# Five loads for each w_in tile, and three neighbouring PSUM banks for each attention chunk

## Chip, core and metric

The kernel runs on one core of a Trainium2 chip. The metric is device time in microseconds. The kernel before the change was run three times: 589.63, 589.65 and 592.54 us, median 589.65 us. All inputs and the output are float32 for the attention part and float64 bit patterns for the two weight matrices, which the kernel reads as pairs of int32 words and turns into float32 itself.

## What is computed

A linear attention with a decay per channel (batch 4, 8 heads, 768 positions, 48 channels a head), whose output, 3072 rows of 384 columns, goes through a two-layer network with the gate h * cos(h):

```python
for t in range(S):
    kt, vt, rt = k[:, :, t], v[:, :, t], r[:, :, t]
    cur = einsum('bhd,bhe->bhde', u[None] * kt, vt)
    y[:, :, t] = einsum('bhd,bhde->bhe', rt, state + cur)
    state = w[None, :, :, None] * state + einsum('bhd,bhe->bhde', kt, vt)
x = y.transpose(0, 2, 1, 3).reshape(B * S, H * D)      # 3072 x 384
h = x @ w_in                                           # 384 x 2048
out = (h * cos(h)) @ w_out                             # 2048 x 384
```

The order of x's 384 columns is free as long as the rows of w_in stand in the same order, since h sums over them. The kernel uses that freedom: x is built transposed, in three thirds of 128 columns, and each third is made of four groups of 32 partitions.

## The kernel before, in words

**Attention.** The sequence is cut into 24 chunks of 128 positions (`chunk`, L631). A chunk loads k, r and v (one DMA each, L647 and L665, pieces of 192 bytes), multiplies r, k and u on POOL (L742, L750, L793), transposes k and r on PE (L711), copies the transposes out with the decay (L768, L779, L788), makes the scores A of eight heads (L818, into two PSUM banks), masks them into SBUF (L824), and makes x transposed from the carried state (L839) and from A and v (L850). It makes k times v for the next state too (L863; the state is updated in L915 to L918). x leaves PSUM twice: ACT rounds it to the reduced type of the matmuls (`xh`, L899), DVE takes the rest (`xl`, L903). Twelve chunks are done before or around the first step of the network (`EARLY = 12`), the others between later steps. The late ones load k and r a second time in another layout (L670), so that DVE can transpose them.

**Banks.** PSUM has eight banks of 512 float32 per partition. Banks 0 to 2 hold output sums and, early, the transposes; 3 to 5 hold h; 5 to 7 serve the attention. An early chunk takes its banks one by one from a pool of five (`B_EARLY`, banks 3 to 7): two for A, then two for x, and one for k times v.

**Network.** 128 steps: a step is one of 16 tiles f of 128 hidden columns for one of eight blocks of 384 rows of x. It has nine matmuls for h (L230: each product is made of three, from high and low parts), then ACT, DVE, ACT, DVE, ACT and DVE in turn (L241, L244, L247, L1017, L1020, L1023) for the gate, and nine matmuls into the output sums (L236). The first four blocks walk over f in groups (f 0 to 1, 2 to 4, 5 to 9, 10 to 15), so that the weights can come in meanwhile; their partial sums are added in DRAM by DMAs from POOL (L1065).

**Weights.** `conv` (L526) turns one tile into high and low parts: f has a w_in tile and a w_out tile, 393 KB of raw words each. A tile is loaded into one of three raw buffers (`R_raw`; the third is r's space, free after the early chunks), converted by ACT L552, DVE L560 and L572, POOL L583, ACT L588 and DVE L593. The raw buffer is free after L583. The w_out tile is one DMA (L461). The w_in tile is eight (L446): x's column order puts two runs of DRAM rows, 16 or 32 rows each and far apart, into neighbouring partitions, so the outermost dimension of the source has two entries:

```python
ap=[[(c1 - c0) * rl, 2], [rl, 16 * n], [1, 2 * P]]
```

In the second half the weights are read once more to look at their range (L456, one DMA for a w_in tile, in the matrix's own row order: 128 rows outermost).

**What sets the order.** Every piece of work is an `op` with an engine, a due time, a cost and buffers. `Plan.order` lays them out by these numbers, and each engine then executes its list strictly in that order. SP issues all loads and the plain stores, one after the other, so a DMA that waits for a free buffer holds up those behind it. Before the first step PE gets dummy matmuls (L1081) where the plan sees a gap.

Of the kernel before, what the change touches and what calls it, by code (L numbers as in the profile page):

```python
# [9 lines left out]
F32 = mybir.dt.float32  # L10
# [153 lines left out]
def kernel(  # L164
# [85 lines left out]
    with ExitStack() as actx:  # L250
# [3 lines left out]
        both = banks.tile([P, 2, 512], F32, name="both")  # L254
        bank = [Tile(both[:, i]) for i in range(2)]
        bank += [Tile(banks.tile([P, 512], F32, name=f"bank{i}")) for i in range(2, 8)]
# [3 lines left out]
        B_TR = [Tile(both)]  # L260
        B_WARM = bank[2]
# [71 lines left out]
        def start_dve():  # L333
# [12 lines left out]
            lambda: nc.sync.dma_start(wr[:, :, 0:D], w.rearrange("(p j) d -> p j d", j=2)),  # L346
# [58 lines left out]
        def tab_copy():  # L405
            pt = b_tab().rearrange("q (p j d) -> q (p j) d", p=NP, j=2)
            nc.scalar.copy(dec_k, pt[:, :, 0:D])
# [26 lines left out]
        def load_raw(i, raw, by_x=False):  # L434
            f, part = divmod(i, 2)
            if part == 0 and by_x:
                rl = 2 * DFF
                for kk in range(NK):
                    g = 0
                    while g < 4:  # L440

                        first = x_columns(kk, g)
                        n = 2 - len(first) + 1
                        (h0, skip0), (h1, skip1) = (x for i in range(n) for _, x in x_columns(kk, g + i))
                        c0, c1 = h0 * D + max(skip0, 0), h1 * D + max(skip1, 0)
                        nc.sync.dma_start(  # L446
                            raw()[32 * g : 32 * (g + n)].rearrange("p (kk f) w -> p kk (f w)", kk=NK)[:, kk],
                            bass.AP(
                                tensor=w_in_w.tensor,
                                offset=w_in_w.offset + c0 * rl + f * P * 2,  # L450
                                ap=[[(c1 - c0) * rl, 2], [rl, 16 * n], [1, 2 * P]],
                            ),
                        )
                        g += n
# [57 lines left out]

        def x_columns(kk, g):

            j, m, which = (
# [3 lines left out]
            )[kk][g]  # L519
            one, two = 4 * m + j, 4 * m + j + 2  # L520
            return (((0, (one, 0)),), ((0, (two, 16)),), ((0, (one, 32)), (16, (two, -16))))[which]
# [86 lines left out]
        for t in range(2):  # L608
            for j in range(2):
                for g in range(4):  # L610
                    some = [(*x, j, kk - j, g) for kk in range(NK) for _, x in x_columns(kk, g) if x[0] % 2 == j]
                    PARTS.append(some[t])

# [17 lines left out]
        def chunk(i, due, xbuf):  # L631
            b, c = i % B, i // B
            first = i < RAW_K
            bk = B_EARLY if i < EARLY else B_ATT
# [6 lines left out]
            Ap = [Buf(bk) for _ in range(2)]  # L641
            A = [Buf(R_A) for _ in range(2)]
            xp = [Buf(bk) for _ in range(2)]
            zp = Buf(bk)

            def load(buf, src):
                return lambda: nc.sync.dma_start(  # L647
                    buf()[:, :, 0:D], src[b, :, c * C : (c + 1) * C, :].rearrange("h t d -> t h d")
                )

# [10 lines left out]
            def rn():  # L661
                return heads(rb) if late else rb()[:, :, 0:D]

            def load_r():
                nc.sync.dma_start(rn(), r[b, :, c * C : (c + 1) * C, :].rearrange("h t d -> t h d"))  # L665

            def load_s(buf, src):
                def part(m, q, n_q, p, n_p, n):
# [5 lines left out]
                            offset=src.offset + ((b * H + 2 * p + j) * S + c * C + 4 * q) * D + d0,  # L674
                            ap=[[4 * D, n_q], [2 * S * D, n_p], [1, n]],
# [73 lines left out]
            def decay_k():  # L749
                n2.tensor_tensor(kb()[:, :, 0:D], kb()[:, :, 0:D], dec_k, op=ALU.mult)  # L750
# [482 lines left out]
```

## Time and profile before

| | |
|---|---|
| median of three runs | 589.65 us |
| the profiled execution | 589.45 us |
| its span, first to last instruction | 587.7 us |
| mean granted TensorE clock | 0.955 |
| PE, DVE, ACT, POOL busy | 527.6, 395.6, 328.4, 178.2 us |
| chain that ended last | PE 63%, DMA 17%, SPq 7%, DVE 5% |

How to read it: PE is TensorE's matmuls and PEld its weight loads, DVE is VectorE, ACT ScalarE, POOL GpSimd; SPq is the queue of SyncE that issues DMAs. "out<-in" names the tile written and those read, "x9" a count. In a row on windows each engine's busy time stands with its number of instructions, then PEclk (the clock that TensorE was granted, 1.00 is full), the mean busy share of the 16 DMA engines, and GB/s. A busy PE is not a PE at full rate, since the ends of matmuls are modelled and a slow clock makes them longer. The chain of waits is followed back from the last instruction; a DMA's piece in it runs from the start of its issue to its landing.

### The profile page before, as it was taken

Reading aid. Unit: us, or ns where it says so; the run is one execution under the profiler, and the core shown is the slowest. Engines: PE = TensorE matmul, PEld = TensorE weight load, DVE = VectorE, ACT = ScalarE, POOL = GpSimd, SP = SyncE. Lnnn points to the kernel's source line nnn. Section 1 sums busy time; section 2 is a strip of 40 time slices with the busy share of each in tenths; the row PEclk is TensorE's granted clock in tenths of the full one; section 3 lists DMA queues with packets and bytes.
Section 4 is the critical chain, followed back from the end, with each engine's and each line's share of the span. In section 5 each row is a group of like instructions: output and inputs, shape, how many; then the busy total and the mean of one; then the engine's idle time right before and its main releaser. Section 6 shows DMA issues by size and latency. Waiting matters only on the chain.

```text
span 587.7 us, 12700 instructions
## 1 busy us (share of the span) xinstructions
PE 527.6 (90%) x4721; PEld 490.9 (84%) x4721; DVE 395.6 (67%) x820; ACT 328.4 (56%) x841; POOL 178.2 (30%) x186
## 2 busy tenths in 40 slices
PE   8979857778668796999999999999999999999994
PEld 5757647667667696999999999999999999999994
DVE  5759865664666485745677688768777877776552
ACT  3768744653545364555456657655755676565442
POOL 6566322123333133411150445043043313300000
PEclk9989959979788987999999999999999999999998
DMA  9687324345344445632536678345726662501001
GB/s 143 113 143 131 72 81 128 107 142 127 87 102 106 105 102 124 124 45 38 95 70 118 124 166 198 83 121 122 190 81 163 163 155 86 150 3 40 2 1 45
DMA packets 114984, 61.66 MB, mean 105 GB/s; under 512 B 78433, under 2 KB 110818, under 8 KB 114914
## 3 DMA queue, kind: packets, MB, share of 16 engines
q1 hardware_dynamic: 109586, 53.50, 37.4%
q0 software_dynamic: 5184, 7.08, 8.6%
q8 instruction: 38, 0.62, 0.5%
q14 instruction: 32, 0.26, 0.1%
q10 hardware_dynamic: 144, 0.20, 0.1%
HBM read 48.96 MB, written 11.80 MB: 103 GB/s over the span
## 4 chain that ended last, share of the span: by engine, by line
PE 63%; DMA 17%; SPq 7%; DVE 5%; POOL 3%; issue 2%; ACT 1%; DVEq 0%; POOLq 0%; ACTq 0%
PE bank L230 26%; PE both L236 18%; PE bank L236 9%; DMA raw<-in_moe_w_in_dram 8%; SPq L446 7%; DMA r_all<-in_moe_w_in_dram 4%; PE bank L818 3%; PE bank L850 3%; DMA r_all<-in_r_dram 2%; DMA raw<-in_moe_w_out_dram 2%; PE bank L839 1%; POOL f L583 1%; DMA r_all<-in_moe_w_out_dram 1%; DMA k<-in_k_dram 1%; PE bank L863 1%
## 5 line engine op out<-in xcount | busy, mean ns | idle before, releaser
L230 PE MATMUL bank<-xh,w_in_hi 128*128 128x384 f32 x384 | 132.5, 345 | 6.8 <-ACT w_in_hi L588 4.1
L230 PE MATMUL bank<-xh,w_in_lo 128*128 128x384 f32 x384 | 131.3, 342 | 1.6 <-DVE w_in_lo L593 1.6
L230 PE MATMUL bank<-xl,w_in_hi 128*128 128x384 f32 x384 | 131.2, 342 | 0.0
L1023 DVE TENSOR_TENSOR gl<-f,gh 128x384 fp32r<-128x384 f32 (+1 forms) x132 | 78.6, 599 | 30.2 <-ACT gh L1020 29.9
L241 ACT ACTIVATE qi<-bank 128x384 int32<-128x384 f32 (+1 forms) x132 | 62.8, 479 | 60.1 <-PE bank L230 59.6
L247 ACT ACTIVATE f<-f 128x384 f32<-128x384 f32 (+1 forms) x132 | 67.3, 513 | 44.6 <-DVE f L244 43.0
L244 DVE SCALAR_TENSOR_TENSOR f<-bank,qi 128x384 f32<-128x384 f32 (+1 forms) x132 | 70.9, 540 | 29.5 <-ACT qi L241 29.1
L236 PE MATMUL both<-w_out_hi,gh 128*128 128x384 f32 x256 | 89.1, 348 | 1.4 <-DVE f L1052 1.1
L1017 DVE TENSOR_TENSOR f<-bank,f 128x384 f32<-128x384 f32 (+1 forms) x132 | 70.9, 540 | 27.3 <-ACT f L247 25.6
L1020 ACT CAST gh<-f 128x384 fp32r<-128x384 f32 (+1 forms) x132 | 65.8, 501 | 42.0 <-DVE f L1017 35.8
L236 PE MATMUL both<-w_out_hi,gl 128*128 128x384 f32 x256 | 88.7, 346 | 0.0
L236 PE MATMUL both<-w_out_lo,gh 128*128 128x384 f32 x256 | 88.3, 345 | 0.0
L230 PEld LDWEIGHTS bank<-xh,w_in_hi 128*128 128x128 f32 x384 | 74.2, 193 | 8.8 <-ACT w_in_hi L588 4.5
L230 PEld LDWEIGHTS bank<-xh,w_in_lo 128*128 128x128 f32 x384 | 73.9, 193 | 2.2 <-DVE w_in_lo L593 2.2
L230 PEld LDWEIGHTS bank<-xl,w_in_hi 128*128 128x128 f32 x384 | 74.1, 193 | 0.0
L236 PE MATMUL bank<-w_out_hi,gl 128*128 128x384 f32 x128 | 45.5, 356 | 20.1 <-DVE gl L1023 20.1
L808 ACT ACTIVATE A<-ident,a 128x128 f32<-128x128 f32 x192 | 59.5, 390 | 4.4 <-DVE a L799 4.2
L236 PE MATMUL bank<-w_out_hi,gh 128*128 128x384 f32 x128 | 45.8, 358 | 11.9 <-ACT f L1050 6.8
L730 POOL TENSOR_TENSOR kT<-kT,decT_k 112x512 f32<-112x512 f32 x12 | 15.7, 1311 | 128.5 <-DVE kT L725 78.4
L236 PEld LDWEIGHTS both<-w_out_hi,gh 128*128 128x128 f32 x256 | 49.5, 193 | 3.1 <-DVE f L1052 1.9
L236 PEld LDWEIGHTS both<-w_out_hi,gl 128*128 128x128 f32 x256 | 49.7, 194 | 0.0
L236 PEld LDWEIGHTS both<-w_out_lo,gh 128*128 128x128 f32 x256 | 49.7, 194 | 0.0
(104 smaller groups left out, 802.6 us busy)
## 6 DMA issues: line engine op xcount, KB each, us to landing
raw<-in_moe_w_out_dram SPq DMA_DIRECT2D x22, 384.0 KB
out_dram<-f POOLq DMA_DIRECT2D x36, 192.0 KB, 5.5
raw<-in_moe_w_in_dram SPq DMA_DIRECT2D x13, 384.0 KB
k<-in_k_dram SPq DMA_DIRECT2D x24, 192.0 KB
v<-in_v_dram SPq DMA_DIRECT2D x24, 192.0 KB
out_dram<-f SPq DMA_DIRECT2D x23, 192.0 KB
r_all<-in_moe_w_out_dram SPq DMA_DIRECT2D x10, 384.0 KB
raw<-in_k_dram SPq DMA_DIRECT2D x31, 96.0 KB
```

The costliest lines, as they stand in the source:

```text
L230: nc.tensor.matmul(ph, a, b_, start=(i == 0), stop=(i == len(mm) - 1))
L236: nc.tensor.matmul(acc, a[:, ts], b_[:, f, :], start=(first and i == 0), stop=(last and i == 2))
L241: nc.scalar.activation(qi, ph, AF.Copy, scale=INV_2PI, bias=0.25)
L244: nc.vector.scalar_tensor_tensor(q, ph, INV_2PI, qi, op0=ALU.mult, op1=ALU.subtract)
L247: nc.scalar.activation(q, q, AF.Sin, scale=TWO_PI, bias=0.5 * math.pi)
L446: nc.sync.dma_start(raw()[32 * g : 32 * (g + n)].rearrange("p (kk f) w -> p kk (f w)", kk=NK)[:, kk], bass.AP(tensor=w_in_w.tensor, offset ...
L808: nc.scalar.activation(A[j]()[:, p, :], ident, AF.Copy, scale=ab()[:, h : h + 1])
L818: nc.tensor.matmul(cube(Ap[j])[:, p, :], kT()[ps, p, :], rT()[ps, p, :], start=True, stop=True)
L850: nc.tensor.matmul(xv(i)[G * g : G * g + G, at, :], vb().rearrange("q h d -> q (h d)")[:, e0 : e0 + G], A[j]()[:, p, :], start=(not c and ...
L1017: nc.vector.tensor_tensor(g()[:, cs], ph()[:, cs], q()[:, cs], op=ALU.mult)
L1020: nc.scalar.copy(gh()[:, cs], g()[:, cs])
L1023: nc.vector.tensor_tensor(gl()[:, cs], g()[:, cs], f32(gh())[:, cs], op=ALU.subtract)
```

## The change

1. x gets a new column order (`x_columns`). Head h sits in half h // 4 of the partitions instead of h % 2. Each w_in tile is loaded by five DMAs, with 64 or 32 partitions as the outermost dimension; two of them carry one third of x, three of them two thirds.
2. All eight banks are one PSUM tile, and a chunk has three neighbouring ones: banks 2 to 4 for odd early chunks up to the ninth, otherwise 5 to 7. The second and third hold A at first; then the three hold a third of x each, in columns 0 to 127. The product of k and v stands in the first of them, in columns 128 to 319.
3. x leaves PSUM in one ACT and one DVE instruction of 128x384, instead of three each.
4. k and r of early chunks are loaded in two DMAs each, four heads a piece (`load_p`), so that the pairs of heads for PE's transposes lie side by side.
5. The dummy matmuls are twice as many with half the columns, in columns 384 to 511 of bank 2.

```diff
-        B_EARLY = bank[5:8] + bank[3:5]
+        B_EARLY = bank[5:8] + bank[2:5]
...
-                rl = 2 * DFF
-                for kk in range(NK):
-                    g = 0
-                    while g < 4:
-                        first = x_columns(kk, g)
-                        n = 2 - len(first) + 1
...
-                                ap=[[(c1 - c0) * rl, 2], [rl, 16 * n], [1, 2 * P]],
...
+                def rows(p0, n, kk, n_kk, c0, dc):
+                    rl = 2 * DFF
+                    dims = [[rl, n], [dc * rl, n_kk], [1, 2 * P]]
+                    nc.sync.dma_start(
+                        raw()[p0 : p0 + n].rearrange("p (kk f) w -> p kk (f w)", kk=NK)[:, kk : kk + 2 * n_kk - 1 : 2],
+                        bass.AP(
+                            tensor=w_in_w.tensor,
+                            offset=w_in_w.offset + c0 * rl + f * P * 2,
+                            ap=dims if n_kk > 1 else [dims[0], dims[2]],
+                        ),
+                    )
+                rows(32, 64, 0, 2, 0, 320)
+                rows(0, 32, 0, 2, 160, 64)
+                rows(96, 32, 0, 2, 128, 64)
+                rows(0, 64, 1, 1, 64, 0)
+                rows(64, 64, 1, 1, 256, 0)
...
-            bk = B_EARLY if i < EARLY else B_ATT
+            b0 = 2 if i % 2 and i < EARLY - 1 else 5
...
-            Ap = [Buf(bk) for _ in range(2)]
+            xp = [Buf([t]) for t in bank[b0 : b0 + 3]]
+            Ap = xp[1:]
...
-            xp = [Buf(bk) for _ in range(2)]
-            zp = Buf(bk)
+            zp = xp[0]
+            x_all = psum[:, b0 : b0 + 3, 0:C]
...
+            def load_p(buf, src):
+                def go():
+                    for j in range(2):
+                        nc.sync.dma_start(
+                            buf()[:, j::2, 0:D],
+                            src[b, j * NP : (j + 1) * NP, c * C : (c + 1) * C, :].rearrange("h t d -> t h d"),
+                        )
+                return go
...
             def x_high():
-                for rows, kk, src in x_parts():
-                    nc.scalar.copy(xbuf()[0][rows, kk], src)
+                nc.scalar.copy(xbuf()[0], x_all)
             def x_low():
-                for rows, kk, src in x_parts():
-                    nc.vector.tensor_tensor(xbuf()[1][rows, kk], src, f32(xbuf()[0])[rows, kk], op=ALU.subtract)
+                nc.vector.tensor_tensor(xbuf()[1], x_all, f32(xbuf()[0]), op=ALU.subtract)
...
-            wp = B_WARM.ap[:, 0:256].rearrange("q (a b) -> q a b", a=2)
-            for _ in range(n):
-                nc.tensor.matmul(wp, warm, warm[:, None, :].to_broadcast([P, 2, P]), start=True, stop=True)
+            for _ in range(2 * n):
+                nc.tensor.matmul(B_WARM, warm, warm, start=True, stop=True)
```

The plan lays the lists out anew. On SP, which issues the loads, this is where the first two early w_in tiles after f = 0 stand before the change: behind the last load of the twelve early chunks (names: k and v are the chunk's tiles, r_all holds r, raw the weights' words).

```order
L647 DMA k_86<-in_k_dram 128x8x48
L665 DMA r_all<-in_r_dram 128x8x48
L647 DMA v_89<-in_v_dram 128x8x48
L446 DMA raw_117<-in_moe_w_in_dram 64x1x256
L446 DMA raw_117<-in_moe_w_in_dram 32x1x256 x2
L446 DMA raw_117<-in_moe_w_in_dram 64x1x256 x2
L446 DMA raw_117<-in_moe_w_in_dram 32x1x256 x2
L446 DMA raw_117<-in_moe_w_in_dram 64x1x256
```

And this is the same place with the change: the two tiles (raw_111 and raw_112) stand between the loads of the last three chunks, five issues each instead of eight.

```order
L442 DMA raw_111<-in_moe_w_in_dram 64x2x256
L442 DMA raw_111<-in_moe_w_in_dram 32x2x256 x2
L442 DMA raw_111<-in_moe_w_in_dram 64x256 x2
L659 DMA k_78<-in_k_dram 128x4x48 x2
L659 DMA r_all<-in_r_dram 128x4x48 x2
L651 DMA v_81<-in_v_dram 128x8x48
L659 DMA r_all<-in_r_dram 128x4x48 x2
L442 DMA raw_112<-in_moe_w_in_dram 64x2x256
L442 DMA raw_112<-in_moe_w_in_dram 32x2x256 x2
L442 DMA raw_112<-in_moe_w_in_dram 64x256 x2
```

So the tiles of f = 1 and 2 are asked for earlier, and the last loads of k, r and v come after them.

On DVE, in the stretch in which weights arrive while steps run, three instructions of a step's gate (L244, L1025, L1031) alternate with three of a tile's conversion (L560, L572, L593). With the change they stand there like this (gl and gh are the gate's parts, f any scratch tile, psum a bank):

```order
L244 SCALAR_TENSOR_TENSOR f_100<-psum,qi_106 128x384
L1060 COPY f_99<-psum 128x384
L1031 TENSOR_TENSOR gl_109<-f_102,gh_107 128x384
L560 TENSOR_SCALAR f_98<-r_all 128x384
L1025 TENSOR_TENSOR f_100<-psum,f_100 128x384
L572 SCALAR_TENSOR_TENSOR f_98<-r_all,f_98 128x384
L593 TENSOR_TENSOR w_out_lo<-f_103,w_out_hi 128x384
```

Before the change the list reads much the same there:

```order
L244 SCALAR_TENSOR_TENSOR f_104<-bank_80,qi_112 128x384
L560 TENSOR_SCALAR f_105<-raw_117 128x384
L1023 TENSOR_TENSOR gl_116<-f_107,gh_114 128x384
L572 SCALAR_TENSOR_TENSOR f_105<-raw_117,f_105 128x384
L593 TENSOR_TENSOR w_out_lo<-f_109,w_out_hi 128x384
L1017 TENSOR_TENSOR f_104<-bank_80,f_104 128x384
```

One tile's conversion goes with one step in both; an L560 that waits for a load holds up the gate instructions behind it.

More of the change, by code (lines that the diff above doesn't have):

```diff
@@ L252 @@
         banks = actx.enter_context(tc.tile_pool(name="banks", bufs=1, space=PSUM))
-        both = banks.tile([P, 2, 512], F32, name="both")
-        bank = [Tile(both[:, i]) for i in range(2)]
-        bank += [Tile(banks.tile([P, 512], F32, name=f"bank{i}")) for i in range(2, 8)]
+        psum = banks.tile([P, 8, 512], F32, name="psum")
+        bank = [Tile(psum[:, i]) for i in range(8)]
         B_ACC, B_H, B_ATT = bank[0:3], bank[3:5], bank[5:8]
         B_HX = bank[3:6]
-        B_EARLY = bank[5:8] + bank[3:5]
-        B_TR = [Tile(both)]
-        B_WARM = bank[2]
+        B_EARLY = bank[5:8] + bank[2:5]
+        B_TR = [Tile(psum[:, 0:2])]
+        B_WARM = bank[2].ap[:, 384:512]
         def ring(name, n, shape, dtype):
@@ L513, in x_columns @@
         def x_columns(kk, g):
-            j, m, which = (
[3 rows of a table removed]
+            return (
[3 rows of a table added]
             )[kk][g]
-            one, two = 4 * m + j, 4 * m + j + 2
-            return (((0, (one, 0)),), ((0, (two, 16)),), ((0, (one, 32)), (16, (two, -16))))[which]
         def conv(i, due, behind=None):
@@ L610 @@
                 for g in range(4):
-                    some = [(*x, j, kk - j, g) for kk in range(NK) for _, x in x_columns(kk, g) if x[0] % 2 == j]
+                    some = [(*x, kk, g) for kk in range(NK) for _, x in x_columns(kk, g) if x[0] // NP == j]
                     PARTS.append(some[t])
+        PARTS = [(*x, x[2:] not in [y[2:] for y in PARTS[:n]]) for n, x in enumerate(PARTS)]
         last_A = [None]
@@ L741, in chunk @@
                 c0,
-                lambda: n0.tensor_tensor(heads(mb), rn(), kb()[:, :, 0:D], op=ALU.mult),
+                lambda: n0.tensor_tensor(
+                    split(heads(mb)), split(heads(rb)) if late else in_turn(rb), in_turn(kb), op=ALU.mult
+                ),
                 [l_r, l_k],
@@ L846, in mm_x @@
                         )
-                for n, (h, skip, i, at, g) in enumerate(PARTS):
-                    p, j = divmod(h, 2)
+                for h, skip, kk, g, new in PARTS:
+                    j, p = divmod(h, NP)
                     e0 = h * DP + skip
                     nc.tensor.matmul(
-                        xv(i)[G * g : G * g + G, at, :],
+                        xp[kk]()[G * g : G * g + G, 0:C],
                         vb().rearrange("q h d -> q (h d)")[:, e0 : e0 + G],
                         A[j]()[:, p, :],
-                        start=(not c and n < 8),
+                        start=(not c and new),
                         stop=True,
```

69 lines of the change are left out of this document (27 added, 42 removed), and 6 rows, old and new, of the table b_fine.

## The prediction

> **What bounds the kernel now.** I read the slices of the page first, then windows, then waits and the chain. PE is short of full from the second slice to the sixteenth (up to about 235 us), its granted clock dips in the same stretch, and the DMA engines are far from full there; afterwards PE is at 9 throughout.
>
> ```profile
> PE   8979857778668796999999999999999999999994
> PEclk9989959979788987999999999999999999999998
> DMA  9687324345344445632536678345726662501001
> ```
>
> The windows put numbers on it: 76.4 to 232 us, from the last product of the last early chunk to the end of the waits, and 340 to 400 us for comparison.
>
> ```profile
> 76.40:232.00 155.60, 113.81 (x559) 106.57 (x552) 92.52 (x193) 76.17 (x173) 46.00 (x44) 0.87 0.42 108
> 340.00:400.00 60.00, 60.00 (x540) 57.01 (x528) 47.25 (x97) 37.45 (x100) 20.45 (x18) 1.00 0.58 136
> ```
>
> In the first, 559 matmuls take 155.6 us; in the second, 540 take 60, among them the short ones of late chunks. What the matmuls of a step cost at full clock is in the chain:
>
> ```profile
> 241.16 1.06 PE both L236 x6
> 243.81 1.56 PE bank L230 x9
> ```
>
> That is 0.173 us for one of L230 (0.177 for L236), so 559 need 559 x 0.173 = 96.9 us. The other 58.7 us are waiting and half clock: PE is idle for 155.6 - 113.8 = 41.8 us, and a mean clock of 0.87 means half speed for a quarter of the time. PE waits in that stretch for the gate's last steps, but those stand on ACT and DVE behind conversions, and the conversions wait for w_in:
>
> ```profile
> PE bank L236 <- DVE gl L1023: 20.1, 8, 6.5
> PE bank L236 <- ACT f L1050: 6.8, 2, 4.1
> ACT raw L552 <- DMA raw<-in_moe_w_in_dram: 32.3, 8, 7.1
> DVE f L560 <- DMA raw<-in_moe_w_in_dram: 16.6, 5, 7.2
> ```
>
> So the loads of w_in set the pace. Their issues on SP, the first and the last of this stretch and one in between, and one load of the range check (L456), which fetches a tile of the same size from the same matrix:
>
> ```profile
> 58.80 4.95 SPq L446 DMA_DIRECT2D raw<-in_moe_w_in_dram  x8
> 89.50 7.38 SPq L446 DMA_DIRECT2D raw<-in_moe_w_in_dram  x8
> 214.50 5.74 SPq L446 DMA_DIRECT2D r_all<-in_moe_w_in_dram  x8
> 386.27 0.37 SPq L456 DMA_DIRECT2D raw<-in_moe_w_in_dram  x1
> ```
>
> From 58.8 to 214.5 us 14 tiles f come in, one in 11.1 us. What the DMA engines do while only w_in loads are in flight, and while the check's load is:
>
> ```profile
> 66.00:68.00 2.00, 2.00 (x70) 1.52 (x74) 1.82 (x7) 0.80 (x2) 0.00 (x0) 1.00 0.14 48
> 388.20:389.20 1.00, 1.00 (x7) 1.00 (x6) 0.56 (x1) 0.80 (x2) 1.00 (x2) 1.00 0.80 274
> ```
>
> With eight loads outstanding the engines are busy to 0.14, which is 2.2 of 16, at 48 GB/s; the same kilobyte rows in the check's order reach 0.80 and 274 GB/s. A w_in tile of 393 KB takes 393/48 = 8.2 us of those two engines, and what is queued behind it there waits too. The two differ in the source's outermost dimension: two runs of rows against 128 rows.
>
> **w_in's loads.** The new loads have 64 or 32 rows outermost, so I expect them to use the engines as the check does. [...]
>
> What a load takes from issue to landing, and the same for w_out tiles, which are 128 rows outermost, once free and once behind w_in loads, is in the chain:
>
> ```profile
> 62.55 0.62 SPq L446
> 63.22 6.71 DMA raw<-in_moe_w_in_dram
> 76.22 2.82 DMA raw<-in_moe_w_out_dram
> 107.42 7.43 DMA raw<-in_moe_w_out_dram
> ```
>
> I take 2.82 us for the landing of the last of five. A w_in tile then saves 3 issues of 0.62 + 0.05 us, 2.0 us, and 6.71 - 2.82 = 3.9 us; a w_out tile behind it up to 7.43 - 2.82 = 4.6 us. Three raw buffers serve 28 tiles in 155.7 us, so one is held 16.7 us; less the mean of 5.9 and 4.6 (5.2 us) it is 11.5 us, and 14 f's come in 14 x 2 x 11.5 / 3 = 107 us, 48 us less.
>
> What is late next in that stretch: PE can't go below 96.9 us. DVE is busy for 92.5 us there, and the change takes nothing from it, since the shorter work on x lies before 76.4 or after 232 us. The highest share of DVE in the windows above at which PE doesn't wait is 47.25/60 = 0.79; at that share 92.5 us need 117 us. So the stretch comes out between 97 and 117 us. I take 112, nearer to DVE's bound, since in DVE's list each step's three gate instructions alternate with three of a conversion. Gain: 155.6 - 112 = 43.6 us. The half clock goes with the long waits.
>
> **The early chunks (up to 76.4 us).** The first w_in tile is loaded amid the loads of k, r and v. Windows of that time and of just before, and a load of r there and before in the chain:
>
> ```profile
> 24.90:32.40 7.50, 6.78 (x149) 5.28 (x145) 4.55 (x11) 3.81 (x13) 0.38 (x1) 1.00 0.53 118
> 15.00:20.00 5.00, 5.00 (x114) 3.51 (x110) 3.38 (x9) 4.14 (x14) 4.54 (x6) 1.00 0.78 134
> 18.07 4.02 DMA r_all<-in_r_dram
> 25.64 6.76 DMA r_all<-in_r_dram
> ```
>
> The engines lose 7.5 x (1 - 0.53/0.78) = 2.4 us; that comes back. Against it, two more w_in tiles now stand ahead of the last chunks' loads: 786 KB at 134 GB/s, 5.9 us. But two steps' h are then done before the last chunk's products, 18 x 0.173 = 3.1 us that the next stretch need not do. Net: -2.4 + 5.9 - 3.1 = +0.4 us; from -2.4 to +5.9.
>
> Splitting k and r adds 24 issues on SP. One costs 0.37 to 0.51 us, and SP has waits for buffers on such loads to hide them:
>
> ```profile
> 56.80 0.37 SPq L647 DMA_DIRECT2D k<-in_k_dram  x1
> 58.19 0.51 SPq L647 DMA_DIRECT2D v<-in_v_dram  x1
> SPq L647 <- PE bank L850: 13.9, 8, 3.3
> ```
>
> 24 x 0.44 = 10.6 us against 13.9 us in this group alone: nothing, and 10.6 us if that cover is gone.
>
> **Banks.** A chunk now holds three banks from its first product of A until x and the state are out, and every second chunk needs the same three. From the chain:
>
> ```profile
> 37.54 2.02 PE bank L818 x15
> 42.66 1.16 PE bank L818 x16
> 44.42 1.01 PE bank L850 x32
> ```
>
> One chunk's A starts at 37.54, the next one's at 42.66, so chunks come every 5.1 us and a set must be free after 10.2. The first chunk's x is done at 45.43, and x leaves in 0.49 + 0.55 us (below): held 8.9 us. It fits, so 0; each us over 10.2 would cost half a us a chunk. [...]
>
> **x out of PSUM.** Three instructions become one. Today's, and two of 384 columns from a bank:
>
> ```profile
> L899 ACT CAST xh<-bank 128x256 fp32r<-128x256 f32 x24 | 8.8, 365 | 7.6 <-PE bank L850 7.0 <-DVE xl L903 0.6
> L899 ACT CAST xh<-bank 128x128 fp32r<-128x128 f32 x24 | 6.4, 266 | 0.6
> L903 DVE TENSOR_TENSOR xl<-bank,xh 128x256 fp32r<-128x256 f32 x24 | 9.9, 415 | 4.1 <-ACT xh L899 4.1
> L903 DVE TENSOR_TENSOR xl<-bank,xh 128x128 fp32r<-128x128 f32 x24 | 7.0, 292 | 0.4
> L241 ACT ACTIVATE qi<-bank 128x384 int32<-128x384 f32 x126 | 61.5, 488 | 59.6 <-PE bank L230 59.1
> L1017 DVE TENSOR_TENSOR f<-bank,f 128x384 f32<-128x384 f32 x126 | 69.5, 552 | 27.3 <-ACT f L247 25.6
> ```
>
> The third, of 64x128, is priced like the 128x128: ACT goes from 0.365 + 2 x 0.266 = 0.90 to 0.49 us, DVE from 0.415 + 2 x 0.292 = 1.00 to 0.55: 0.41 and 0.45 us a chunk. Twelve chunks lie where PE never waits (340 to 400 us above): nothing. In the early ones it shortens the hold, which has room: nothing, at best 6 x 0.86 = 5 us. The dummy matmuls have as many columns as before and stand in planned gaps: nothing.
>
> **Sum**, against the profiled execution's 589.45 us (0.2 below the median): 589.45 - 43.6 + 0.4 = 546.2, so **546 us**.
>
> **Rivals.**
>
> (a) The raw buffers stay the bound. If landing and hold shrink by half as much as priced, 14.1 us a buffer, 14 f's take 132 us instead of 107; the stretch ends some 22 us later than forecast: 568 us. For it: L552 and L560 are in-order and POOL's L583 stands behind stores; against it: those queues are late today because the loads are.
>
> (b) The loads don't spread, and only the issues go. The engines then still need 8.2 us a tile at 48 GB/s; 3 issues less give up to 14 x 2.0 = 28 us if all lie on the path and nothing if the transfer covers them: 561 to 589, middle 575 us. Against it: 0.80 busy in the check's load of the same rows.
>
> (c) Slower: two sets of banks hold up the early chunks. It decides where a set is held over 10.2 us; to eat the whole gain it must be held over 17.5 us. At 18.5 us twelve chunks lose 12 x 8.3 / 2 = 50 us, which gives 596 us. Against it: 8.9 us above. For it: a chunk's end waits for ACT and DVE, which also serve other chunks and conversions.
>
> **How the numbers follow.** Forecast 0.67, (a) 0.20, (b) 0.08, (c) 0.05. A measurement of this kernel can tell about 0.5% (3 us) from no change. Of (b) 0.03 lies within that, so faster is 0.67 + 0.20 + 0.05 = 0.92, same 0.03, slower 0.05. The range's low end is the stretch at PE's bound with the early gain: 589.45 - 58.7 - 2.4 = 528. Its high end takes in (a): 568 us and 2 for its rounding, 570. Outside lie (c), most of (b), and part of (a).
>
> **What would show it.** Right: with w_in loads in flight the DMA share is several times 0.14; a w_in tile has five issues, some 3.3 us in all, and lands about 3 us after the last; PE at 9 and clock near 1.0 from about 85 us on; the steps reach the state of 232 us by about 190; idle time before L552 and L560 mostly gone; 340 us to the end as before. Wrong: windows at 48 GB/s again (b); PE still waiting for gl with L552 idle for DMA (a); the last L850 of an early chunk far beyond 80 us (c). If DVE is at 0.9 or more in that stretch, 112 was too high; if PE waits for gl with DVE at 0.7 and no load late, the order itself is the limit, and the forecast's mechanism falls short.

## The result and the profile after

| | before | after |
|---|---|---|
| median | 589.94 us (4 runs) | 534.90 us (4 runs, 534.28 to 537.02) |
| ratio, 95% interval | 1 | 0.9065, 0.9028 to 0.9101 |
| profiled execution, its span | 589.45, 587.7 us | 535.15, 533.2 us |
| mean granted clock | 0.955 | 0.992 |
| PE, DVE, ACT, POOL busy | 527.6, 395.6, 328.4, 178.2 us | 512.1, 387.9, 318.8, 180.0 us |

Faster by 55 us where 43 were forecast; the time lies in the range, on its low side. The slices of the page show where it came from: PE is at 9 from the sixth slice on, but for the eleventh at 8 (a slice is 13.3 us; before, it was at 9 from the seventeenth), and the clock stays at 9 after the fifth.

```profile
PE   7997799999899999999999999999999999999995
PEclk9998899999999999999999999999999999999999
```

The same stretch in the view of windows, once over its old length and once up to where nearly all weights are in. The columns are the length, then busy time with instruction count of PE, PEld, DVE, ACT and POOL, then clock, DMA share and GB/s.

```profile
76.40:232.00 155.60, 153.92 (x949) 150.77 (x948) 127.82 (x249) 105.00 (x237) 61.17 (x60) 1.00 0.58 132
76.40:178.00 101.60, 99.92 (x640) 96.77 (x639) 92.73 (x185) 73.83 (x168) 43.71 (x43) 1.00 0.62 154
83.00:84.00 1.00, 1.00 (x52) 0.80 (x56) 0.79 (x2) 0.43 (x1) 1.00 (x1) 1.00 0.54 182
```

Where 559 matmuls took 155.6 us, 949 are done now. In the first 101.6 us DVE is busy for 92.7 us, about as long as in 155.6 us before, at a share of 0.91, and PE still hardly waits. The third row is a microsecond in which loads of one w_in tile alone are in flight (the one issued from 81.17 us on, below): 182 GB/s at a DMA share of 0.54, where 48 GB/s at 0.14 stood before.

SP's timeline has these w_in tiles: f = 3 before the change, then f = 3, 4 and 15 with it:

```profile
82.64 4.95 SPq L446 DMA_DIRECT2D r_all<-in_moe_w_in_dram  x8
```

```profile
73.11 3.12 SPq L442 DMA_DIRECT2D raw<-in_moe_w_in_dram  x5
81.17 2.89 SPq L442 DMA_DIRECT2D r_all<-in_moe_w_in_dram  x5
166.81 2.92 SPq L442 DMA_DIRECT2D raw<-in_moe_w_in_dram  x5
```

A tile now takes 2.89 us to issue where SP isn't held up, instead of 4.95. From f = 3 to f = 15 one w_in tile is asked for every 7.8 us (73.11 to 166.81), where it was 11.0 (82.64 to 214.50); the prediction's sum over the raw buffers gave 107 us for 14, 7.7 each. In the table of waits L552's wait for w_in is nearly gone (the first row, up to 180 us; before, 32.3 us), and two waits are new (the second row over the whole span, the third up to 180 us):

```profile
ACT raw L552 <- DMA raw<-in_moe_w_in_dram: 1.3, 1, 1.3
DVE zc L925 <- ACT xh L908: 12.9, 10, 2.0
PE psum L1088 <- DVE xl L911: 2.8, 3, 2.4
```

The second is the state's update waiting for ACT's copy of x, which reads the same bank; the third is a dummy matmul behind x's other copy. The chain of waits runs through PE for 85% of the span (63% before), and in the stretch it is step after step without a gap:

```profile
97.69 1.58 PE psum L236 x9
99.27 1.56 PE psum L230 x9
```

Two marks in PE's timeline are needed below, the last product for x of an early chunk (L850 before, L868 now; the row gives least, middle and greatest ns, then first and last start) and the 33rd step of the network, which ends the old stretch. First before, then after:

```profile
L850 PE MATMUL bank<-A,v x32: 421/421/421, 74.8 to 76.4; 128*32 128x128 f32 x32
L230 PE MATMUL bank<-xh,w_in_hi x3: 522/522/522, 231.4 to 233.3; 128*128 128x384 f32 x3
```

```profile
L868 PE MATMUL psum<-A,v x32: 272/273/298, 83.5 to 84.3; 128*32 128x128 f32 x32
L230 PE MATMUL psum<-xh,w_in_hi x3: 332/336/337, 178.8 to 179.9; 128*128 128x384 f32 x3
```

The first goes from 76.4 to 84.3 us, the second from 231.4 to 178.8. What follows the second takes 356.3 us before (587.7 - 231.4) and 354.4 now (533.2 - 178.8).

### The profile page after: what moved, and what is told of

Same layout as the page of the kernel before. It is cut to its first block, busy times and chain, and to the rows that moved or that the text cites. A ratio compares the mean times of both kernels' runs of the same rounds, so it can differ in the third digit from the quotient of the medians.

```text
span 533.2 us, 12662 instructions
## 1 busy us (share of the span) xinstructions
PE 512.1 (96%) x4790; PEld 485.3 (91%) x4790; DVE 387.9 (73%) x772; ACT 318.8 (60%) x793; POOL 180.0 (34%) x186
## 4 chain that ended last, share of the span: by engine, by line
PE 85%; DVE 7%; issue 2%; ACT 2%; DMA 2%; SPq 1%; POOL 0%; DVEq 0%; ACTq 0%; POOLq 0%
PE psum L236 36%; PE psum L230 34%; PE psum L839 5%; PE psum L868 4%; PE psum L857 2%; PE psum L882 2%; PE psum L1088 1%; DVE A L845 1%; DVE rT L789 1%; DVE gl L1031 1%; SPq L442 1%; DMA raw<-in_moe_w_in_dram 1%; DVE xl L911 1%; PE psum L730 1%; DMA r_all<-in_moe_w_in_dram 1%
## 5 line engine op out<-in xcount | busy, mean ns | idle before, releaser
L236 PE MATMUL psum<-w_out_hi,gh 128*128 128x384 f32 x384 | 131.9, 343 | 0.8 <-ACT f L1058 0.8
L236 PE MATMUL psum<-w_out_hi,gl 128*128 128x384 f32 x384 | 130.2, 339 | 0.8 <-DVE gl L1031 0.8
L230 PE MATMUL psum<-xh,w_in_hi 128*128 128x384 f32 x384 | 129.5, 337 | 0.1
L236 PE MATMUL psum<-w_out_lo,gh 128*128 128x384 f32 x384 | 129.6, 337 | 0.0
L230 PE MATMUL psum<-xh,w_in_lo 128*128 128x384 f32 x384 | 129.4, 337 | 0.0
L230 PE MATMUL psum<-xl,w_in_hi 128*128 128x384 f32 x384 | 128.9, 336 | 0.0
L1031 DVE TENSOR_TENSOR gl<-f,gh 128x384 fp32r<-128x384 f32 (+1 forms) x132 | 81.1, 616 | 27.5 <-ACT gh L1028 27.1
L244 DVE SCALAR_TENSOR_TENSOR f<-psum,qi 128x384 f32<-128x384 f32 (+1 forms) x132 | 70.8, 539 | 30.6 <-ACT qi L241 30.2
L1025 DVE TENSOR_TENSOR f<-psum,f 128x384 f32<-128x384 f32 (+1 forms) x132 | 70.8, 539 | 25.8 <-ACT f L247 24.6
L236 PEld LDWEIGHTS psum<-w_out_hi,gl 128*128 128x128 f32 x384 | 72.1, 188 | 1.8 <-DVE gl L1031 1.6
L230 PEld LDWEIGHTS psum<-xh,w_in_hi 128*128 128x128 f32 x384 | 72.1, 188 | 1.3 <-issue 0.6
L230 PEld LDWEIGHTS psum<-xl,w_in_hi 128*128 128x128 f32 x384 | 72.2, 188 | 0.0
L230 PEld LDWEIGHTS psum<-xh,w_in_lo 128*128 128x128 f32 x384 | 72.2, 188 | 0.0
L845 DVE COPY_PREDICATED A<-upper,psum 128x512 f32<-128x512 int32 x48 | 33.7, 736 | 19.8 <-PE psum L839 17.5
L1073 POOL DMA_DIRECT2D out_dram<-f x36 | 32.3, 1142 | 44.5 <-ACT f L1058 42.2
```

Source lines behind the costliest of these rows:

```text
L230: nc.tensor.matmul(ph, a, b_, start=(i == 0), stop=(i == len(mm) - 1))
L236: nc.tensor.matmul(acc, a[:, ts], b_[:, f, :], start=(first and i == 0), stop=(last and i == 2))
L244: nc.vector.scalar_tensor_tensor(q, ph, INV_2PI, qi, op0=ALU.mult, op1=ALU.subtract)
L845: return lambda: nc.vector.copy_predicated(A[j](), upper[:, None, :].to_broadcast([P, NP, C]), cube(Ap[j]))
L1025: nc.vector.tensor_tensor(g()[:, cs], ph()[:, cs], q()[:, cs], op=ALU.mult)
L1031: nc.vector.tensor_tensor(gl()[:, cs], g()[:, cs], f32(gh())[:, cs], op=ALU.subtract)
```

## Experiments

Each ran with the kernel before beside it. In microseconds, with the ratio to before:

| run | median | ratio, 95% interval |
|---|---|---|
| after | 534.9 | 0.9065, 0.9028 to 0.9101 |
| five_on_two | 536.6 | 0.9077, 0.9048 to 0.9106 |
| eight_spread | 544.5 | 0.9209, 0.9176 to 0.9243 |
| eight_on_two | 588.7 | 0.9954, 0.9931 to 0.9977 |
| before_sixteen_loads | 570.8 | 0.9653, 0.9612 to 0.9693 |
| three_copies_out | 534.1 | 0.9023, 0.8983 to 0.9063 |
| one_set_of_banks | 548.6 | 0.9270, 0.9243 to 0.9298 |
| w_in_after_chunks | 544.1 | 0.9211, 0.9186 to 0.9235 |
| four_pieces_of_k_and_r | 545.8 | 0.9252, 0.9236 to 0.9267 |
| dve_twice | 543.2 | 0.9176, 0.9149 to 0.9202 |
| dve_four_times | 569.9 | 0.9640, 0.9610 to 0.9670 |
| w_lo_on_pool | 538.2 | 0.9114, 0.9097 to 0.9130 |
| three_blocks_first | 531.7 | 0.8996, 0.8973 to 0.9019 |

The two marks of the section above cut each profiled execution into parts. In microseconds, with the number of steps whose h matmuls (L230) are done before the last product of the last early chunk:

| run | that product | 33rd step | between them | steps' h before |
|---|---|---|---|---|
| before | 76.4 | 231.4 | 155.0 | 1 |
| after | 84.3 | 178.8 | 94.5 | 3 |
| five_on_two | 89.3 | 183.7 | 94.4 | 3 |
| eight_spread | 86.4 | 190.2 | 103.8 | 3 |
| eight_on_two | 94.0 | 232.6 | 138.6 | 3 |
| before_sixteen_loads | 81.6 | 214.1 | 132.5 | 1 |
| one_set_of_banks | 104.2 | 190.0 | 85.8 | 6 |
| w_in_after_chunks | 83.9 | 188.8 | 104.9 | 1 |
| four_pieces_of_k_and_r | 96.3 | 190.9 | 94.6 | 3 |
| dve_twice | 87.5 | 186.6 | 99.1 | 3 |
| dve_four_times | 93.8 | 210.7 | 116.9 | 3 |
| w_lo_on_pool | 98.3 | 183.5 | 85.2 | 6 |

The theory: w_in's loads set the pace because they kept only 0.14 of the 16 DMA engines busy (before, 66 to 68 us, as much as 2.2 engines), and spreading them over more lets the stretch fall to the next bound. The rivals: it is the number of issues, or the earlier request, or the layout of the banks.

### Spread or number of issues: five_on_two, eight_spread, eight_on_two, before_sixteen_loads

**five_on_two** cuts each of the five loads into two halves by its source:

```diff
-                            ap=dims if n_kk > 1 else [dims[0], dims[2]],
+                            ap=[[n // 2 * rl, 2], [rl, n // 2], *(dims[1:] if n_kk > 1 else dims[2:])],
```

> The changed kernel, but the source of each of the five w_in loads has two half runs as its outermost dimension again; issues, order and everything else stay. If the gain comes from the loads' spreading over all DMA engines, a tile takes about 8 us of two engines again (DMA share near 0.14 and 48 GB/s while only w_in loads are in flight) and the time is 561 to 589 us, most likely about 577. If it comes from three issues less a tile, from the banks or from the new order, the time stays near 535 us.

536.6 us. The two halves lie behind each other in DRAM and were joined again when the program was built, so it is instruction for instruction that of after. It tells nothing of the spreading; it is a second measurement of the change, and its profile shows how much two executions of one program differ. Between the two marks they take 94.4 and 94.5 us, but the early chunks end at 89.3 instead of 84.3 us. From 10 to 15 us PE was granted 0.64 of its clock here and all of it in the profile of after, and did 44 matmuls instead of 72. First five_on_two, then after:

```profile
10.00:15.00 5.00, 3.75 (x44) 3.18 (x41) 2.09 (x4) 2.70 (x9) 3.08 (x4) 0.64 0.93 128
```

```profile
10.00:15.00 5.00, 3.75 (x72) 3.25 (x69) 3.30 (x6) 2.80 (x9) 4.26 (x5) 1.00 1.04 133
```

So one profile gives the end of the early chunks to some 5 us only.

**eight_spread** takes the old number of loads, each with its partitions outermost:

```diff
-                rows(32, 64, 0, 2, 0, 320)
-                rows(0, 32, 0, 2, 160, 64)
-                rows(96, 32, 0, 2, 128, 64)
+                for kk in (0, 2):
+                    rows(32, 64, kk, 1, 160 * kk, 0)
+                    rows(0, 32, kk, 1, 160 + 32 * kk, 0)
+                    rows(96, 32, kk, 1, 128 + 32 * kk, 0)
```

> The changed kernel with eight w_in loads a tile as before (64 or 32 KB each), all with 64 or 32 partitions outermost. If spreading is all that counts and SP has room, 535 to 539 us. If the three issues less a tile lie on the path as the prediction priced them (2.0 us a tile, 14 tiles), up to 28 us more: about 555 to 563 us.

544.5 us. A row of SP's timeline:

```profile
83.23 4.81 SPq L442 DMA_DIRECT2D r_all<-in_moe_w_in_dram  x8
```

Three issues more cost 1.9 us of SP's time a tile and 8 to 10 us in all, which lies between the two forecasts. That is a sixth of the gain, and between the marks it is 9.3 us (103.8 - 94.5). The prediction's sum over the raw buffers makes the same of them: 2.0 us on every second tile is 1.0 us on the mean hold, times 28 tiles over 3 buffers, 9.3 us. If that sum is what holds here, the raw buffers have no slack left after the change: they bind at nearly the same place as PE.

**eight_on_two** leaves all that as it is, sizes, places and order too, and differs from eight_spread in w_in's loads alone. It lets each load take its rows as two runs that can't be joined, the even and the odd ones:

```diff
-                            ap=dims if n_kk > 1 else [dims[0], dims[2]],
+                            ap=[[rl, 2], [2 * rl, n // 2], [1, 2 * P]],
```

> The eight loads a w_in tile of eight_spread (544.5 us) with the same sizes and places, but each takes its rows as two runs, the even and the odd ones, so that the source's outermost dimension has two entries; the two runs are not contiguous, so they cannot be joined. (It puts w_in's rows into another order than x's columns, so h is of other products; nothing else differs.) If the change's gain comes from spreading the transfers over the engines, the windows with w_in loads alone fall back to 0.14 busy at some 48 GB/s, landing goes from about 2.5 to some 6 us, and the stretch after the early chunks goes back to about 150 us: 575 to 595 us. If it comes from the order of the loads, the banks or the earlier request, it stays at 540 to 548 us.

588.7 us. The windows of a time with only w_in loads in flight and of the old stretch:

```profile
62.00:64.00 2.00, 2.00 (x36) 1.77 (x32) 1.26 (x3) 0.47 (x2) 0.72 (x1) 0.50 0.13 46
76.40:232.00 155.60, 120.65 (x762) 110.57 (x755) 93.83 (x196) 76.81 (x179) 44.59 (x44) 0.89 0.41 106
```

A tile's issue in SP's timeline, then a landing in the chain:

```profile
99.16 5.95 SPq L442 DMA_DIRECT2D raw<-in_moe_w_in_dram  x8
```

```profile
51.27 6.49 DMA raw<-in_moe_w_in_dram
```

And two rows of the waits up to 190 us:

```profile
ACT raw L553 <- DMA raw<-in_moe_w_in_dram: 17.6, 5, 4.6
DVE f L561 <- DMA raw<-in_moe_w_in_dram: 11.6, 4, 4.6
```

These are the signs of before again: 46 GB/s at 0.13, landings of 6.5 us, conversions waiting for w_in, half clock. So of the 55 us about 44 (0.9954 - 0.9209 of 590) come from the spreading alone, 8 from the three issues, and 3 from all else together: the earlier request, the banks, the single copy and the split of k and r. This division holds for taking things away in this order: the 3 us were measured with the loads at a share of 0.13, and with spread loads the order of the early requests alone is worth 8 to 9 us (w_in_after_chunks).

**before_sixteen_loads** goes the other way: the kernel before, each of the eight loads cut into its two runs, to spread them, which doubles the issues.

```diff
-                        nc.sync.dma_start(
-                            raw()[32 * g : 32 * (g + n)]...,
-                            ... ap=[[(c1 - c0) * rl, 2], [rl, 16 * n], [1, 2 * P]],
+                        for e, c0 in enumerate((h0 * D + max(skip0, 0), h1 * D + max(skip1, 0))):
+                            p0 = 32 * g + 16 * n * e
+                            nc.sync.dma_start(
+                                raw()[p0 : p0 + 16 * n]...,
+                                ... ap=[[rl, 16 * n], [1, 2 * P]],
```

> The kernel before, its column order, banks and early chunks kept; each of the eight w_in loads is cut into its two runs, so sixteen loads a tile, each with 32 or 16 rows outermost. If spreading counts, the loads no longer run at 48 GB/s, but SP needs about 16 x 0.6 = 10 us a tile, which is about the pace of before (11 us): 560 to 580 us. If SP's issues hide, 540 us. If the number of loads is what counts, over 600 us.

570.8 us: 20 of the 55 us without the new order of x's columns. What holds it now is, by these rows, SP: it issues for 116 of the 132.5 us between the marks, 103 of them w_in's loads. A tile in its timeline:

```profile
86.31 8.19 SPq L447 DMA_DIRECT2D r_all<-in_moe_w_in_dram  x16
```

The window of the stretch:

```profile
76.40:216.00 139.60, 114.31 (x640) 105.29 (x641) 96.57 (x203) 79.84 (x186) 48.28 (x47) 0.91 0.52 124
```

A tile needs 8.19 us of issues, as long as its transfer took before (393 KB at 48 GB/s). The column order is what makes few loads and spread loads possible together (five loads a tile at a share of 0.54, after).

### What bounds the stretch afterwards: dve_twice, dve_four_times, w_lo_on_pool

The prediction's 112 us rested on DVE. The first two issue L560 two and four times for each weight tile; a repeat only writes the same words again (the cut shows two):

```diff
-                lambda: nc.vector.tensor_scalar(
-                    ai(), hw(), 3, 0x3FFFFFF8, op0=ALU.logical_shift_left, op1=ALU.bitwise_and
-                ),
+                lambda: [
+                    nc.vector.tensor_scalar(
+                        ai(), hw(), 3, 0x3FFFFFF8, op0=ALU.logical_shift_left, op1=ALU.bitwise_and
+                    )
+                    for _ in range(2)
+                ],
```

> L560 issued twice for each weight tile (the second writes the same words again): 26 in the stretch from 76.4 to 178 us by 0.45 us are 11.7 us more for DVE, 92.7 + 11.7 = 104.4 us of work where the stretch takes 101.6. If DVE binds only when it is full, the stretch grows by some 3 to 5 us and the time is 537 to 541 us. If PE cannot go on at full rate with DVE above 0.79, as the prediction had it, the stretch needs 132 us: about 565 us.

> L560 issued four times: 35 us more for DVE in the same stretch, 128 us of work. If DVE binds only when full: the stretch takes some 130 us, 28 more, 560 to 566 us with DVE at 0.97 or more there. If 0.79 is the share at which it binds: 162 us, about 595 us. If DVE's order matters (a gate's steps behind conversions), PE's waits for gl grow well before DVE is full: between the two.

543.2 and 569.9 us. The windows between the two marks, of after, with two and with four:

```profile
84.30:178.80 94.50, 92.82 (x534) 90.79 (x525) 86.23 (x172) 69.10 (x156) 40.92 (x40) 1.00 0.64 159
```

```profile
87.50:186.60 99.10, 94.09 (x534) 90.55 (x527) 94.13 (x196) 68.43 (x156) 40.42 (x41) 1.00 0.61 151
```

```profile
93.80:210.70 116.90, 101.33 (x534) 92.20 (x527) 111.59 (x246) 68.77 (x155) 40.08 (x40) 0.97 0.53 129
```

With four, the groups of L560 (here L561) between 76 and 205 us, and a wait between 76.4 and 200 us:

```profile
L561 DVE TENSOR_SCALAR f<-raw 128x384 int32<-128x384 int32 x68 | 25.6, 376 | 1.8
...
L561 DVE TENSOR_SCALAR f<-r_all 128x384 int32<-128x384 int32 x36 | 13.1, 364 | 0.9
```

```profile
PE psum L236 <- DVE gl L1034: 6.7, 10, 1.3
```

For the same 534 matmuls DVE's share goes from 0.91 to 0.95 (94.13 of 99.10 us) and stays there (111.59 of 116.90), however much it is given, and PE's falls from 0.98 to 0.95 and 0.87. That is DVE's bound here. So the change leaves the stretch where both engines are nearly full: PE at 0.98, and DVE 0.04 below its own bound.

At 0.372 us (38.7 us over 104) four issues instead of one are 32 x 3 x 0.372 = 35.7 us more for the 32 tiles, and the time rose by 35.0: in the profiles 22.4 us between the marks, 9.5 before them and some 3 behind. Two instead of one are 12 us, and it rose by 7 to 8, 4.6 of them between the marks. Both times lie 2 to 4 us above the range expected for a DVE that binds when full, which had the whole cost in the stretch.

**w_lo_on_pool** takes work from DVE instead:

```diff
-                DVE,
+                DVE if part else POOL,
...
-                lambda: nc.vector.tensor_tensor(lo, av(), f32(hi), op=ALU.subtract),
+                lambda: (nc.vector if part else nc.gpsimd).tensor_tensor(lo, av(), f32(hi), op=ALU.subtract),
```

> L593 of the w_in tiles (0.564 us each, 14 in the stretch) goes from DVE to POOL, which is busy for 43.7 of the 101.6 us there. DVE loses 7.9 us of work in the stretch. If PE's own work is the bound there (PE busy 99.9 of 101.6 us), nothing is won: 533 to 538 us. If DVE at 0.91 still holds PE, some 5 us are won: 528 to 531 us. POOL and DVE may slow each other; then 538 us or more.

538.2 us, not faster (2 to 3 us above after and its repeat, but its interval overlaps with both of theirs). DVE is relieved, and PE is not fuller for it; the window between the marks has DVE at 0.89 and PE at 0.98 again:

```profile
98.30:183.50 85.20, 83.45 (x494) 82.28 (x485) 75.70 (x136) 58.88 (x133) 46.51 (x47) 1.00 0.62 149
```

The plan also laid the early chunks out otherwise for it (six steps' h come before their last product, which starts at 98.3 us instead of 84.3), so this run alone doesn't show that DVE's load was no limit; it agrees with it. So does one_set_of_banks below: with six steps' h done before, too, and DVE not relieved, it takes 85.8 us between the marks against 85.2 here.

### The early chunks: w_in_after_chunks, four_pieces_of_k_and_r, one_set_of_banks, three_copies_out

**w_in_after_chunks** holds the planner's early weights back:

```diff
-HOLD = ()
+HOLD = (24, 24, 9, 9, 9)
```

> The change, but the tile of f = 1 is not asked for ahead of the early chunks' last loads: on SP it stands behind them again. The prediction priced the two tiles between those loads at 5.9 us lost and 3.1 us won back by steps done earlier. If that is right, the last early chunk ends some 3 to 6 us earlier than 84.3 us, the steps begin later, and the time is within 3 us of after: 532 to 538 us. If the early request is worth more than that, as PE's bound from 76 to 178 us suggests (a step not done early is 3.1 us of PE work that stays to be done), it is 538 to 545 us.

544.1 us, 8 to 9 us slower. The edit did more than was meant. f = 1 and f = 2 now come behind the last chunks' loads, but other tiles took their places ahead of them: w_out of f = 2 (46.28) and w_in of f = 3 (55.78), 393 KB each. SP's timeline, where the last row is f = 1 and f = 2, then PE's wait up to 190 us:

```profile
46.28 0.51 SPq L462 DMA_DIRECT2D raw<-in_moe_w_out_dram  x1
...
55.78 2.91 SPq L442 DMA_DIRECT2D raw<-in_moe_w_in_dram  x5
...
75.45 6.68 SPq L442 DMA_DIRECT2D raw<-in_moe_w_in_dram  x10
```

```profile
PE psum L230 <- ACT w_in_hi L588: 4.0, 1, 4.0
```

So the run shows what it is worth to ask for the right tiles early, 8 to 9 us: the steps begin with a wait, and the stretch is 10.4 us longer, 3.1 of them the h of two steps that wasn't done before. It doesn't show what two tiles ahead of the loads cost the chunks, since as many bytes stand there. They end at 83.9 us; the clock from 10 to 15 us was 0.68, nearly as low as in five_on_two (89.3 us, with those two steps' h done by then).

**four_pieces_of_k_and_r** doubles what the change added to SP:

```diff
                     for j in range(2):
-                        nc.sync.dma_start(
-                            buf()[:, j::2, 0:D],
-                            src[b, j * NP : (j + 1) * NP, ...
+                        for m in range(2):
+                            nc.sync.dma_start(
+                                buf()[:, j + NP * m : j + NP * m + NP - 1 : 2, 0:D],
+                                src[b, j * NP + m * NP // 2 : j * NP + (m + 1) * NP // 2, ...
```

> k and r of early chunks are loaded in four DMAs each instead of two: 48 more issues on SP before 70 us, by 0.46 to 0.53 us each 22 to 25 us. The prediction put the 24 that the change adds at nothing, since SP waits for buffers there. If that cover holds for twice as many, the time is 534 to 538 us. If SP has no gap left where it issues without a pause (19 to 46 us), the some 20 new issues that fall there delay the chunks behind by about 10 us: 542 to 550 us, and the 24 of the change cost about 5 us as well. If every one lies on the path: 556 to 560 us.

545.8 us. The last product of the early chunks (here L869) comes 12 us later than in the profile of after, 7 later than in that of its repeat, and the stretch behind it is as long as in both:

```profile
L869 PE MATMUL psum<-A,v x32: 272/273/297, 95.5 to 96.3; 128*32 128x128 f32 x32
```

And these rows are from SP's timeline of after:

```profile
29.99 1.06 SPq L659 DMA_DIRECT2D k<-in_k_dram  x2
31.16 2.13 SPq L659 DMA_DIRECT2D r_all<-in_r_dram  x2
33.38 0.68 SPq L651 DMA_DIRECT2D v<-in_v_dram  x1
```

Each row begins about 0.1 us behind the end of the one before it, and so it goes from 23.5 to 40 us: SP has no pause there. 48 more issues cost 10 to 11 us, 0.22 us each; at that price the change's own 24 cost about 5 us (an estimate; loading k and r whole in the new order was not tried).

**one_set_of_banks** gives all early chunks the banks 5 to 7:

```diff
-            b0 = 2 if i % 2 and i < EARLY - 1 else 5
+            b0 = 5
```

> All early chunks use banks 5 to 7, none banks 2 to 4. [...] With one set the ten chunks that changed sets come 9.2 instead of 5.1 us apart: 40 us more, about 575 us. If a set is held for less than thought, or the loads of k, r and v set the pace of the early chunks anyway, 537 to 550 us. If the set with two is already the limit (chunks wait for banks now), more than 40 us.

548.6 us: 11 to 14 us slower, where 40 would follow from a set held for 9.2 us. The last two early chunks' products:

```profile
L868 PE MATMUL psum<-A,v x64: 272/273/297, 95.5 to 104.2; 128*32 128x128 f32 x64
```

The last starts 20 us later than in after. The stretch behind it is 8.7 us shorter, as three more steps' h are done meanwhile. In after a chunk's A begins at 35.78 us (L839), and its set is free once DVE has copied x at 43.48 (PE's timeline, then DVE's):

```profile
35.78 1.16 PE L839 MATMUL psum<-rT,kT 48*128 48x128 f32 x16
```

```profile
41.15 0.36 DVE L925 TENSOR_TENSOR zc<-psum,zc 112x192 f32<-112x192 f32 x1 [0.78 <-ACT xh L908]
...
42.94 0.54 DVE L911 TENSOR_TENSOR xl<-psum,xh 128x384 fp32r<-128x384 f32 x1
```

That is 7.7 us held, with the state's update waiting for ACT's copy inside it and rT of the next chunk between it and x's copy. Over the twelve early chunks it is 6.8 to 9.7 us, in the repeat (five_on_two) up to 10.6.

**three_copies_out** undoes the single copies:

```diff
-                nc.scalar.copy(xbuf()[0], x_all)
+                for kk in range(NK):
+                    nc.scalar.copy(xbuf()[0][:, kk], x_all[:, kk])
...
-                nc.vector.tensor_tensor(xbuf()[1], x_all, f32(xbuf()[0]), op=ALU.subtract)
+                for kk in range(NK):
+                    nc.vector.tensor_tensor(xbuf()[1][:, kk], x_all[:, kk], f32(xbuf()[0])[:, kk], op=ALU.subtract)
```

> The changed kernel, x leaves PSUM in three ACT and three DVE instructions of 128x128 a chunk (a bank each) instead of one of each. The prediction put this at nothing, at most 5 us: 535 to 540 us. If the shorter work on ACT and DVE (0.86 us a chunk) was on the path of all 24 chunks, 20 us more: 555 us.

534.1 us, the same. First its groups, then those of after:

```profile
L913 DVE TENSOR_TENSOR xl<-psum,xh 128x128 fp32r<-128x128 f32 x72 | 16.2, 279 | 1.6 <-ACT xh L909 1.6
L909 ACT CAST xh<-psum 128x128 fp32r<-128x128 f32 x72 | 14.3, 271 | 18.7 <-PE psum L882 9.5 <-PE psum L868 6.7 <-DVE zc L927 2.2
```

```profile
L911 DVE TENSOR_TENSOR xl<-psum,xh 128x384 fp32r<-128x384 f32 x24 | 13.2, 549 | 3.6 <-ACT xh L908 3.6
L908 ACT CAST xh<-psum 128x384 fp32r<-128x384 f32 x24 | 11.4, 474 | 22.0 <-PE psum L882 10.0 <-PE psum L868 9.8 <-DVE zc L925 2.1
```

Three us of DVE and three of ACT are saved, and none of it shows in the time.

### A version that is a little faster: three_blocks_first

With the weights on time, the longest stretch in which PE isn't full is that of the early chunks. This version does nine of them first and walks three blocks over f in groups:

```diff
-GRP = 4
+GRP = 3
...
-EARLY = 12
+EARLY = 9
```

> Three blocks of x walk over f in groups instead of four, after nine early chunks instead of twelve; three chunks move into the later part. PE's work is the same, but its idle time and dummies lie before 84 us, and that stretch gets shorter by some 15 us. If the weights then come in time, PE stays full and the time falls by 5 to 15 us: 520 to 530 us. If conversions now pace the steps (28 tiles and as many gates in fewer us of PE work: DVE above 0.95), it is 533 to 545 us.

531.7 us, 0.8996 (0.8973 to 0.9019), below both measurements of the change (0.9028 to 0.9101 and 0.9048 to 0.9106) by 3 to 5 us, where 5 to 15 were expected. The interval of three_copies_out reaches into it. PE is at 8 or 9 from the second slice on and waits for the gate's last step between 76 and 190 us (its slices, its window of the stretch and that wait):

```profile
PE   6999899999999999999999999999999999999994
```

```profile
76.40:178.00 101.60, 96.98 (x632) 93.87 (x631) 93.03 (x179) 70.69 (x167) 54.04 (x51) 1.00 0.76 170
```

```profile
PE psum L236 <- DVE gl L1031: 4.3, 5, 1.2
```

It wins early and gives part of it back where DVE is at 0.92. Whether the chunks that moved into the later part cost something as well stays open.

## Why the prediction was right, and where its sizes were off

**What bounded the kernel: right.** w_in's loads kept 0.14 of the DMA engines busy. eight_on_two differs from eight_spread (544.5 us) in the access pattern of these loads alone; it is back at 588.7 us and at 0.13. Why two entries outermost give this share, no run shows.

**The loads spread: right.** A tile's issue fell by 2.1 us (4.95 to 2.89), a load of a w_in tile lands a median 2.4 us after its issue where it is one of 64 KB into a raw buffer (the page's group of DMA issues; 2.82 forecast for the last of a tile), and from f = 3 on a tile is asked for every 7.8 us, as the raw buffers' sum had it (7.7). Rival (b) is out: 182 GB/s with one tile's loads alone, and three issues less are worth 8 to 10 us, not 28.

**The stretch: the term that was mis-sized.** 112 us were forecast. The failing step is "the highest share of DVE in the windows above at which PE doesn't wait is 0.79; at that share 92.5 us need 117 us". A share at which nothing waits is no bound: in that window DVE simply had no more to do. DVE went to 0.91 with PE at 0.98, and its bound is 0.95, by dve_twice and dve_four_times. At 0.95, 92.5 us need 97.4, so PE and DVE bind at nearly the same place, and the stretch ended near PE's 97. Counted from the last product of the last early chunk to the 33rd step it fell from 155.0 us (76.4 to 231.4) to 94.5 (84.3 to 178.8); with the 3.1 us of h done beforehand that is 97.6, and the gain 57.4 us instead of 43.6. The repeat of the change gives 94.4 for the 94.5. The prediction named the sign itself: DVE at 0.9 or more means that 112 was too high.

**The early chunks: off by 4.4 us in the two profiles, and wrong in one part.** They end 7.9 us later (84.3 against 76.4), and with 3.1 us of h done earlier that is +4.8 instead of +0.4; the repeat of the change would make it +9.8, so the size is known to some 5 us only. One part that the working had at nothing is not nothing: the 24 issues. "SP has waits for buffers on such loads to hide them" took waits from the whole early part as cover for issues that fall where SP has none (23 to 40 us). That is about 5 us, by the price that four_pieces_of_k_and_r gives. The +5.9 for two w_in tiles ahead of the loads and the -2.4 for the engines given back were not measured: no run takes the tiles away without putting as many bytes in their place. How the rest of the delay divides between these tiles, the state's wait and the dummies' isn't settled.

**Banks: right at nothing, for the size forecast.** Held 6.8 to 9.7 us (up to 10.6 in the repeat), forecast 8.9, limit 10.2. The state's update did wait for ACT's copy of x, 12.9 us over ten times (three of them, 4.2 us, up to 90 us), and ACT takes 0.474 us for it. The 9.2 us with which one_set_of_banks was reckoned lies about midway between 8.9 and 8.9 with ACT's copy (0.49 us) on top; that addition was the author's estimate, and no run shows it by itself: what they show is the 6.8 to 9.7 us held. Rival (c) would have needed 17.5 us; even one set instead of two costs only 11 to 14 us.

**x out of PSUM, dummies: nothing, as said.** The dummies' wait for x's copy, 2.8 us, was not foreseen; with 2.4 us of it in one place in the early part, it is within what stays open there.

**The rest of the span** gave 1.9 us that the sum didn't have; no run separates it. The terms as the two profiles have them: -57.4 + 4.8 - 1.9 = -54.5, the difference of the spans (587.7 - 533.2).

Rival (a), raw buffers still the bound at 132 us, is out: L552 waits 1.3 us for w_in up to 180 us. Its 568 should read 566 us, since 132 is 20 us over 112, not 22. But by eight_spread the raw buffers have no slack either: what the sum makes 1.0 us more of hold cost 9.3 us between the marks.

## What to carry to other kernels

Look at the DMA share while one kind of load alone is in flight: here it was 0.13 to 0.14 with eight loads outstanding, and the access pattern decided it (588.7 us in eight_on_two, 544.5 in eight_spread). The order in which a contraction runs can be free to mend it, as that of x's columns was. When a bound is lifted, price the next one by what that engine can do, not by the highest share that a comfortable window happens to show: add work to the engine and see where the other one starts to fall. Cover for an added issue counts only at the place where the issue stands in its queue. And before a difference of a few us in one part is explained, look at that part in a second execution of the same program.

## What was not expected of the hardware

- One program, two executions: the clock granted from 10 to 15 us was 1.00 in one and 0.64 in the other, and the early chunks ended 5 us apart (after and five_on_two).
- With two entries in the outermost dimension of the source, the even and the odd rows, w_in's loads kept 0.13 of the DMA engines busy and the kernel took 588.7 us; with as many loads of as many rows in one run it took 544.5 (eight_on_two, eight_spread). A cut into two halves that lie behind each other never reached the chip, since they were joined when the program was built (five_on_two).
- In after, where SP issued without a pause (23.5 to 40 us), an issue took 0.46 us for k (0.92 us for two at 23.48) and up to 1.07 us for r (2.13 us for two at 31.16); later it took 0.37 us for v (at 51.93 and at 63.09).
- On POOL, L593 took 1.22 us on the mean between 76 and 178 us (w_lo_on_pool; 1.03 in the median over the run), against 0.56 us on DVE there (after), and POOL's L583 on the words in r's space took 1.52 us on the mean beside it, against 1.20 (after).
